# Reordering the Strassen sums in a two-layer gelu kernel: a late gelu, T3 behind T4, and an earlier split of a weight piece

## The chip, the cores and the metric

The kernel runs on one core of a Trainium2 chip. The metric is device time in microseconds (us), the median of several runs; the lower the better. TensorE is called PE (PEld is its weight load), VectorE DVE, ScalarE ACT, GpSimd POOL and SyncE SP.

## The reference, cut to what matters

A causal convolution of seven taps per head runs over the sequence, and its result goes through two matrix products with a gelu between.

```python
# x: (8, 4096, 192), weight: (8 heads, 7 taps); taps softmaxed per head
out = np.einsum('hk,bskhg->bshg', w, x_unf)        # the convolution
x = out.reshape(32768, 192)
h = x @ w_in                                       # 192 -> 2048
g = h * (1.0 / (1.0 + np.exp(-1.702 * h)))         # the gelu
return (g @ w_out).astype(np.float32)              # 2048 -> 192
```

All is in float32. The weights come as 64-bit floats: the kernel takes them apart as pairs of 32-bit words and puts float32 values together ("split", "join" and "round" below).

## The kernel before

The tokens are cut into 32 large blocks ("big"), each of two steps: a first one (s even) and a second one (s odd). The first block is done in a plainer way (`first_steps`); the other 31 run in a loop of pairs of steps, and nearly all of the time is spent there. A pair has four stages: the hidden layer of the first step, that of the second, the output of the first, the output of the second. DVE computes the convolution of a later block in the spaces between: `work(t)` takes the next pieces of that from a list, as many as fit into t us by the kernel's own estimates.

Both layers are computed by schemes that trade products for sums. The hidden layer takes 21 products ("terms") where the plain way takes 24. Each goes into one of four PSUM buffers (called x, y, z and sums here), with pieces copied aside (k15 to k20, all in one SBUF tile `room`). The output layer is a Strassen scheme: seven products (A11 B11, A12 B21, S4 B22, A22 T4, S1 T1, S2 T2, S3 T3) in place of eight. A and S come from w_out. B11 to B22 are gelu outputs in the tile `g`, and T1 to T4 are differences of them, made by DVE. T1 and T2 lie in the memory of k15, k20, k19 and k18. T3 overwrites B12 and T4 overwrites B21. Each has two halves (u = 0, 1).

```python
def half(s, b, u):
    if b in (T1, T2):
        return room[:, 2 * (b - T1) + u, :].rearrange("p (f t) -> p f t", t=T)
    return g[:, s % 2, u, b, :, :]
...
def sum_g(s, u, dst, terms):                                            # L494
    vec.tensor_sub(half(s, dst, u), half(s, terms[0], u), half(s, terms[1], u))
def sum_1(s, u): sum_g(s, u, T1, (B12, B11))
def sum_2(s, u): sum_g(s, u, T2, (B22, T1))
def sum_3(s, u): sum_g(s, u, T3, (B22, B12))
def sum_4(s, u): sum_g(s, u, T4, (T2, B21))
```

The hidden layer of a step; `pe(slot, *terms)` issues the matmuls of terms (each 2 x 2 matmuls of 64 rows, seen as eight records in the profile: L472), and `gelu` is an ACT instruction (L487):

```python
def hidden(s, x, z, y, sums, work, fetch):
    second = s % 2
    ...
    if second:
        pe(z, 7, first=True)
    pe(sums, 12)
    act.copy(k15, sums)                       # L524
    pe(x, 5, 17)
    gelu(s, B11, 0, x)
    if not second:
        pe(z, 7, first=True)
    pe(sums, 0)
    act.copy(k16, sums)                       # L530
    work(3.2 if second else 1.5)
    pe(y, 6, 14, first=True)
    vec.tensor_sub(x, z, k15)                 # L533
    work(2.6)
    pe(sums, 13)
    act.copy(k19, sums)                       # L536
    pe(x, 2)
    act.copy(k18, x)                          # L538
    pe(z, 11)
    pe(sums, 20, 10)
    vec.tensor_sub(k15, y, k19)               # L541
    gelu(s, B12, 0, sums)
    pe(x, 4)
    act.copy(k20, x)                          # L544
    vec.tensor_sub(k19, z, k19)               # L545
    work(1.1)
    gelu(s, B22, 1, k19)
    gelu(s, B22, 0, k15)
    pe(y, 8)
    pe(sums, 1, 9, first=True)
    pe(y, 15)
    if second:
        sum_1(s - 1, 0)
    else:
        work(1.2)
    work(1.1)
    vec.tensor_add(k20, k20, sums)            # L557
    vec.tensor_sub(k16, y, k16)               # L558
    gelu(s, B11, 1, k20)
    pe(x, 18)
    gelu(s, B21, 1, x)
    fetch()                                   # term 16 of the next step, into z
    if not second:
        act.copy(y, z)                        # L565
    gelu(s, B21, 0, k16)
    if second:
        sum_2(s - 1, 0)
    else:
        work(1.2)
    pe(sums, 3, 19)
    work(0.7)
    vec.tensor_add(k18, k18, sums)            # L573
    gelu(s, B12, 1, k18)                      # the "last gelu"
```

The output of a step. `product2` is 64 matmuls (L582) in 16 groups of four: three column tiles of one product and, as the fourth, a third of another product. `quarters` (L598) makes the last third of A22 T4. The results are added up and turned (L618) for the store.

```python
def output(s, ra, rb, work, between=None):
    ...
    p1, p3c = product2(s, ra, 0, (A11, B11), (S4, B22, 0))
    act.copy(u1, p1)
    act.copy(chunk(p3, 0), p3c)
    sum_1(s, 1)
    sum_2(s, 1)
    sum_3(s, 0)
    sum_3(s, 1)
    work(0.7)
    p2, p3c = product2(s, rb, 0, (A12, B21), (S4, B22, 1))
    act.copy(chunk(p3, 1), p3c)               # L654
    vec.tensor_add(u2, u1, p2)                # L655
    out.turn(0, 0, u2)
    sum_4(s, 0)
    sum_4(s, 1)
    p6, p3c = product2(s, ra, 1, (S2, T2), (S4, B22, 2))
    act.copy(chunk(p3, 2), p3c)
    vec.tensor_add(u2, u1, p6)                # L661
    work(3.2)
    ...
    p5, p4c = product2(s, rb, 1, (S1, T1), (A22, T4, 0))
    q = quarters(s, rb, 0, A22, T4, 2)
    ...                                       # L667 to L672, a turn
    if s % 2:
        work(1.5)
    else:
        sum_1(s + 1, 0)
        sum_2(s + 1, 0)
    p7, p4c = product2(s, ra, 0, (S3, T3), (A22, T4, 1))
    ...                                       # L680 to L684, two turns, the store
```

At the start, the four pieces of w_in are taken apart by DVE (L273, L274, L295, L300, L304) and ACT (L284 and, by the value of LATE, three steps L289 to L291 or, with one more clamp on DVE, L276, one step L287), between the first plain products:

```python
LATE = 4                                      # pieces from here on take the clamp on DVE
...
    gelu(0, B11, 0, slots[0])
    gelu(0, B12, 0, sums)
    for m, n, slot, b in quarters[2:]:
        plain(0, 0, m, n, slot)
        gelu(0, b, 0, slot)
    cross(0, 1, C11, C21, nc.gpsimd)
    split_piece(3)
    split_rest(3)
    round_w_in(2)
    load_w_out(2)
    split_piece(4)
    split_rest(4)
    join_piece(3)
    round_w_in(3)
    load_w_out(3)
```

The whole kernel:

Of the kernel before, what the change touches and what calls it, by code (L numbers as in the profile page):

```python
# [15 lines left out]
def kernel(  # L16
# [72 lines left out]
    def load_x(big):  # L89


        p, c = divmod(big, CHUNKS)
        xin = xins[big] = xin_pool.tile([P, 2, NJ, XW], F32, name="xin")
        if c == 0:
            nc.gpsimd.memset(xin[0:R, :, 0, :], 0.0)
        for n in range(2):
            for o in range(2):
                j = 1 if c == 0 and o == 0 else 0
                t = c * TOK + o * T + (j - 1) * Q
                for v in range(2):  # L100
                    q0 = o * R + v * Q
                    nc.sync.dma_start(
                        out=xin[q0 : q0 + Q, n, j:NJ, :],
                        in_=x_v[n, p, t : t + (NJ - j) * Q, v * Q : v * Q + XW].rearrange(
                            "(j i) d -> i j d", i=Q
                        ),
                    )
# [3 lines left out]
    sums = psum.tile([P, 2, TOK], F32, name="sums")  # L111
# [3 lines left out]
    B11, B12, B21, B22, T1, T2 = range(6)  # L115
# [6 lines left out]
    k15, k20, k19, k18, k16 = (room[:, i, :].rearrange("p (h n) -> p h n", h=2) for i in range(5))  # L122
# [138 lines left out]
    def words(i):  # L261
        w = raw[i % NW].rearrange("p (n w) -> p n w", w=2)
        return (w[:, :, 0], w[:, :, 1]) + tuple(sets[SET[i]])


    LATE = 4

    def split_piece(i):

        lo, hi, m, l, e = words(i)  # L270
        ef = e.bitcast(F32)

        vec.tensor_scalar(m, hi, 0xFFFFF, 1 << 20, op0=ALU.bitwise_and, op1=ALU.bitwise_or)  # L273
        vec.tensor_scalar(e, hi, 20, 0x7FF, op0=ALU.logical_shift_right, op1=ALU.bitwise_and)  # L274
        if i >= LATE:
            vec.tensor_scalar(  # L276
                ef, e, float(LOW + 255), float(LOW), op0=ALU.min, op1=ALU.max
            )

    def split_rest(i):  # L280

        lo, hi, m, l, e = words(i)
        ef = e.bitcast(F32)
        act.activation(l.bitcast(F32), lo, AF.Copy, scale=2.0**-32)  # L284

        if i >= LATE:
            act.activation(e, ef, AF.Identity, bias=bias[:, 3:4], scale=2.0**23)  # L287
        else:
            act.activation(ef, e, AF.Relu, bias=bias[:, 0:1])  # L289
            act.activation(ef, ef, AF.Relu, bias=bias[:, 1:2], scale=-1.0)  # L290
            act.activation(e, ef, AF.Identity, bias=bias[:, 2:3], scale=-(2.0**23))  # L291
# [40 lines left out]
    def load_w_out(i):  # L332
        nc.sync.dma_start(
            out=raw[i].rearrange("p (c d) -> p c d", c=CW),
            in_=w_out_v[:, i * CW : (i + 1) * CW, :],
        )
# [149 lines left out]
    def gelu(s, b, u, src):  # L486
        act.activation(  # L487
            half(s, b, u).rearrange("p f t -> p (f t)"),
            src.rearrange("p h n -> p (h n)"),
            AF.Gelu_apprx_sigmoid,  # L490
        )

    def sum_g(s, u, dst, terms):
        vec.tensor_sub(half(s, dst, u), half(s, terms[0], u), half(s, terms[1], u))  # L494

    def sum_1(s, u):
        sum_g(s, u, T1, (B12, B11))

    def sum_2(s, u):
        sum_g(s, u, T2, (B22, T1))  # L500

    def sum_3(s, u):
        sum_g(s, u, T3, (B22, B12))
# [6 lines left out]
        for k in ks:  # L510
            product1(slot, NC * (2 * u + m) + k, 2 * k + n, s, k == first)

    def hidden(s, x, z, y, sums, work, fetch):

        second = s % 2

        def pe(slot, *ts, first=False):
            terms(s, slot, *ts, first=first)
# [9 lines that stand above are left out]
            pe(z, 7, first=True)  # L528
        pe(sums, 0)
        act.copy(k16, sums)  # L530
        work(3.2 if second else 1.5)
        pe(y, 6, 14, first=True)
        vec.tensor_sub(x, z, k15)  # L533
# [15 lines that stand above are left out]
        pe(y, 8)  # L549
        pe(sums, 1, 9, first=True)  # L550
        pe(y, 15)
        if second:
            sum_1(s - 1, 0)
        else:
            work(1.2)
        work(1.1)
        vec.tensor_add(k20, k20, sums)  # L557
        vec.tensor_sub(k16, y, k16)  # L558
        gelu(s, B11, 1, k20)
        pe(x, 18)  # L560
        gelu(s, B21, 1, x)
        fetch()
        if not second:

            act.copy(y, z)  # L565
        gelu(s, B21, 0, k16)
        if second:
            sum_2(s - 1, 0)
        else:
            work(1.2)  # L570
        pe(sums, 3, 19)
        work(0.7)
        vec.tensor_add(k18, k18, sums)  # L573
        gelu(s, B12, 1, k18)

    def product2(s, slot, bank, ab, last, first=True):

# [59 lines left out]
    def chunk(t, c):  # L637
        return t[c * Q : (c + 1) * Q, :]

    def output(s, ra, rb, work, between=None):  # L640

        out = Out(s)
        u1, u2, p3, p4 = us

        p1, p3c = product2(s, ra, 0, (A11, B11), (S4, B22, 0))
        act.copy(u1, p1)
        act.copy(chunk(p3, 0), p3c)
        sum_1(s, 1)
        sum_2(s, 1)
        sum_3(s, 0)  # L650
        sum_3(s, 1)
        work(0.7)
        p2, p3c = product2(s, rb, 0, (A12, B21), (S4, B22, 1))
        act.copy(chunk(p3, 1), p3c)  # L654
        vec.tensor_add(u2, u1, p2)  # L655
# [3 lines that stand above are left out]
        p6, p3c = product2(s, ra, 1, (S2, T2), (S4, B22, 2))  # L659
        act.copy(chunk(p3, 2), p3c)  # L660
        vec.tensor_add(u2, u1, p6)  # L661
        work(3.2)
        if between:
            between()
        p5, p4c = product2(s, rb, 1, (S1, T1), (A22, T4, 0))
        q = quarters(s, rb, 0, A22, T4, 2)
        act.copy(chunk(p4, 0), p4c)  # L667
        vec.tensor_add(u1, u2, p5)
        act.copy(chunk(p4, 2), q[2])
        vec.tensor_add(p3, u1, p3)  # L670
        for l in (0, 1, 3):
            vec.tensor_add(chunk(p4, 2), chunk(p4, 2), q[l])  # L672
        out.turn(0, 1, p3)
# [6 lines that stand above are left out]
        act.copy(chunk(p4, 1), p4c)  # L680
        vec.tensor_add(u1, u1, p7)
        vec.tensor_add(u2, u2, p7)
        out.turn(1, 1, u1)
        vec.tensor_sub(u2, u2, p4)  # L684
        out.turn(1, 0, u2)
        out.store()
# [3 lines left out]
    def work(us):  # L690
        while todo and todo[0][1] <= us + 0.2:
            us -= todo[0][1]
            todo.pop(0)[2]()
# [28 lines left out]
    def first_steps(fetch):  # L722

        first, second = slice(0, 1), slice(1, 2)
# [49 lines left out]
        plain(0, 0, 0, 0, slots[0], (2,))  # L774
        plain(0, 0, 0, 1, sums, (2, 0), 1)
        gelu(0, B11, 0, slots[0])
        gelu(0, B12, 0, sums)
        for m, n, slot, b in quarters[2:]:
            plain(0, 0, m, n, slot)
            gelu(0, b, 0, slot)  # L780
        cross(0, 1, C11, C21, nc.gpsimd)
        split_piece(3)
        split_rest(3)
        round_w_in(2)
        load_w_out(2)
        split_piece(4)
        split_rest(4)
        join_piece(3)
        round_w_in(3)
        load_w_out(3)  # L790
        load_x(1)

        def piece_5():
# [61 lines left out]
    def fetch(s, slot):  # L855

        need(f"first {s // 2}")
        terms(s, slot, 16, first=True)
# [6 lines left out]
    x, y, z = slots[2], slots[1], slots[0]  # L865
    for big in range(1, N_BIG):
        s = 2 * big
        more = big + 1 < N_BIG
        hidden(s, x, z, y, sums, work, lambda: fetch(s + 1, z))
        give(s)  # L870
        x, z, y, sums = z, x, sums, y
        hidden(s + 1, x, z, y, sums, work, lambda: fetch(s + 2, z) if more else None)
        if more:
            act.copy(sums, z)
        output(s, y, x, work)
        if more:
            need(f"all {big + 1}")
            cross(big + 1, 1)
        if big + 2 < N_BIG:
            todo.extend(prepare(big + 2))  # L880
        output(s + 1, x, y, work)
        x, y, z = z, x, y
# [30 lines left out]
```

## Time and profile before

| | |
|---|---|
| time, median of 3 runs | 2425.85 us (2425.5 to 2426.86) |
| span in the profile | 2424.7 us |
| PE busy | 2391.2 us |
| DVE busy | 2018.8 us |
| ACT busy | 1052.7 us |
| granted PE clock, mean | 0.999 |

How to read it: an engine's row gives its busy time, its share of the span and its number of instructions. A row of waits says which engine and line waited for which other, then the total, the number of times and the longest, in us. A row of a time line gives start, duration, engine, line, operation, and output <- inputs; a bracket at its end holds the idle time before it and what ended it. A row of the chain of waits gives start, duration, and what was running. Matmuls are pipelined, and their ends are modelled. L-numbers are lines of the kernel, as marked in the code above; in the changed kernel they shift by a line or two.

### The profile page before, as it was taken

How to read it: one execution, taken by the hardware profiler on the slowest of the kernel's cores; microseconds unless marked ns; L12 is line 12 of the kernel's file. 1: busy time of each engine (PE TensorE's matmuls, PEld its weight loads, DVE VectorE, ACT ScalarE, POOL GpSimd, SP SyncE). 2: the span in 40 equal slices, each digit the busy share in tenths (PEclk: the TensorE clock that was granted, in tenths of full speed). 3: DMA queues.
4: the chain of work that ended last, by engine and by line, in shares of the span. 5: the costliest groups of instructions: out<-in, count | busy, mean ns of one | idle time of the engine just before them, and what ended most of it. 6: DMA issues, size and time to landing. Idle time of an engine off the chain costs nothing.

```text
span 2424.7 us, 71778 instructions
## 1 busy us (share of the span) xinstructions
PE 2391.2 (99%) x32602; PEld 1755.3 (72%) x32602; DVE 2018.8 (83%) x2853; ACT 1052.7 (43%) x1369; POOL 9.1 (0%) x30
## 2 busy tenths in 40 slices
PE   9999999999999999999999999999999999999998
PEld 8667776677776777766777667777677776677765
DVE  7888888888888889888888888888888988888866
ACT  6235443344433455333544334443345533354433
POOL 1000000000000000000000000000000000000000
PEclk9999999999999999999999999999999999999999
DMA  7421332212323123322133231232312323213210
GB/s 163 84 52 35 64 67 56 62 35 51 67 56 65 37 47 67 62 58 50 36 64 67 56 62 32 54 67 54 65 37 46 67 60 61 52 34 65 43 29 15
DMA packets 195824, 135.90 MB, mean 56 GB/s; under 512 B 110752, under 2 KB 186016, under 8 KB 193536
## 3 DMA queue, kind: packets, MB, share of 16 engines
q1 hardware_dynamic: 194912, 131.06, 26.6%
q8 instruction: 255, 4.18, 0.8%
q14 instruction: 49, 0.40, 0.1%
q10 hardware_dynamic: 560, 0.13, 0.0%
q0 software_dynamic: 48, 0.13, 0.0%
HBM read 53.15 MB, written 25.17 MB: 32 GB/s over the span
## 4 chain that ended last, share of the span: by engine, by line
PE 73%; DVE 15%; ACT 6%; issue 3%; DMA 2%; SPq 1%; POOL 0%; DVEq 0%; POOLq 0%; ACTq 0%
PE slot L472 30%; PE slot L582 20%; PE sums L472 11%; PE sums L582 9%; DVE room L494 4%; ACT g L487 4%; DVE g L494 3%; DMA out_dram<-osbs 2%; DVE osbs L618 2%; PE slot L598 2%; DVE room L557 1%; ACT room L544 1%; DVE room L672 1%; DVE xt L396 1%; SPq L633 1%
## 5 line engine op out<-in xcount | busy, mean ns | idle before, releaser
L472 PE MATMUL slot<-crossed,w_in_s 64*128 64x256 f32 x3940 | 904.9, 378 | 7.3 <-DVE room L557 7.3
L472 PE MATMUL slot<-f,w_in_s 64*128 64x256 f32 x3940 | 905.1, 378 | 1.6 <-DVE w_in_s L304 1.6
L582 PE MATMUL slot<-g,w_out_s 128*32 128x256 f32 x9792 | 781.5, 379 | 9.0 <-DVE g L494 9.0
L472 PEld LDWEIGHTS slot<-crossed,w_in_s 64*128 64x128 f32 x3940 | 731.4, 187 | 60.0 <-DVE room L557 15.7
L472 PEld LDWEIGHTS slot<-f,w_in_s 64*128 64x128 f32 x3940 | 731.5, 187 | 54.7 <-issue 9.0
L582 PEld LDWEIGHTS slot<-g,w_out_s 128*32 128x32 f32 x9792 | 422.8, 110 | 227.6 <-DVE g L494 18.5
L413 DVE SCALAR_TENSOR_TENSOR f<-xt,cw,f 128x512 f32<-128x512 f32 (+1 forms) x570 | 421.9, 740 | 15.6
L582 PE MATMUL sums<-g,w_out_s 128*32 128x256 f32 x4704 | 385.6, 379 | 5.1 <-DVE g L494 5.1
L487 ACT ACTIVATE g<-room 128x1024 f32<-128x1024 f32 x310 | 321.3, 1059 | 132.6 <-DVE room L557 105.2
L472 PE MATMUL sums<-crossed,w_in_s 64*128 64x256 f32 x1460 | 360.6, 378 | 2.7 <-DVE room L557 2.7
L472 PE MATMUL sums<-f,w_in_s 64*128 64x256 f32 x1460 | 360.6, 378 | 0.0
L582 PE MATMUL slot<-room,w_out_s 128*32 128x256 f32 x4032 | 305.2, 379 | 0.0
L472 PEld LDWEIGHTS sums<-crossed,w_in_s 64*128 64x128 f32 x1460 | 270.5, 187 | 25.7 <-DVE room L557 6.7
L582 PEld LDWEIGHTS sums<-g,w_out_s 128*32 128x32 f32 x4704 | 205.0, 110 | 111.9 <-DVE g L494 10.2
L472 PEld LDWEIGHTS sums<-f,w_in_s 64*128 64x128 f32 x1460 | 270.6, 187 | 18.7 <-issue 4.5
L494 DVE TENSOR_TENSOR room<-g 128x1024 f32<-128x1024 f32 x126 | 151.2, 1200 | 106.1 <-ACT g L487 106.1
L582 PEld LDWEIGHTS slot<-room,w_out_s 128*32 128x32 f32 x4032 | 163.7, 110 | 91.6 <-issue 0.3
L487 ACT ACTIVATE g<-slot 128x1024 f32<-128x1024 f32 x157 | 159.8, 1018 | 97.9 <-PE slot L472 97.6
L494 DVE TENSOR_TENSOR room<-g,room 128x1024 f32<-128x1024 f32 x126 | 154.1, 1223 | 5.5
L582 PE MATMUL sums<-room,w_out_s 128*32 128x256 f32 x2016 | 154.5, 379 | 0.0
L494 DVE TENSOR_TENSOR g<-g 128x1024 f32<-128x1024 f32 x126 | 148.3, 1218 | 0.0
L494 DVE TENSOR_TENSOR g<-room,g 128x1024 f32<-128x1024 f32 x126 | 145.8, 1195 | 0.0
(170 smaller groups left out, 1943.7 us busy)
## 6 DMA issues: line engine op xcount, KB each, us to landing
xin<-in_x_dram SPq DMA_DIRECT2D x240, 180.0 KB, 5.0
crossed<-f SPq DMA_DIRECT2D x31, 832.0 KB, 5.9
out_dram<-osbs SPq DMA_DIRECT2D x382, 64.0 KB, 1.8
crossed<-f SPq DMA_DIRECT2D x31, 448.0 KB, 3.8
crossed<-f SPq DMA_DIRECT2D x31, 256.0 KB, 2.9
crossed<-f SPq DMA_DIRECT2D x31, 128.0 KB, 2.2
xin<-in_x_dram SPq DMA_DIRECT2D x16, 160.0 KB, 4.3
g<-in_moe_w_in_dram SPq DMA_DIRECT2D x4, 384.0 KB, 13.1
```

What stands on the lines that cost most here:

```text
L396: vec.transpose(xts[big][:, c, ns, :].rearrange("p n (j t) -> p (n j) t", t=Q), xins[big][:, ns, :, :].rearrange("p n j d -> p (n j) d")[: ...
L413: vec.scalar_tensor_tensor(out=dst, in0=src, scalar=tap, in1=dst, op0=ALU.mult, op1=ALU.add)
L472: nc.tensor.matmul(slot[:, h, j * T : (j + 1) * T], w_in_s[halves[h], a, j * P : (j + 1) * P], (f if h == o else crossed)[halves[h], b, :] ...
L487: act.activation(half(s, b, u).rearrange("p f t -> p (f t)"), src.rearrange("p h n -> p (h n)"), AF.Gelu_apprx_sigmoid,)
L494: vec.tensor_sub(half(s, dst, u), half(s, terms[0], u), half(s, terms[1], u))
L544: act.copy(k20, x)
L557: vec.tensor_add(k20, k20, sums)
L582: nc.tensor.matmul(dst[l * Q : (l + 1) * Q, :], w_out_s[:, a, j, c * Q : (c + 1) * Q], half(s, b, j // (NK // NU))[:, j % (NK // NU), :], ...
L598: nc.tensor.matmul(dst[l], w_out_s[:, a, j, c * Q : (c + 1) * Q], half(s, b, j // (NK // NU))[:, j % (NK // NU), :], start=(i == 0), stop= ...
L618: vec.transpose(self.osb[:, n, :, m * Q : (m + 1) * Q], src.rearrange("p (j t) -> p j t", t=Q),)
L633: (act if c % 2 and self.s == N_ST - 1 else nc.sync).dma_start(out=rows[c], in_=self.osb[c * Q : (c + 1) * Q, n, :, :])
L672: vec.tensor_add(chunk(p4, 2), chunk(p4, 2), q[l])
```

## The change

The sums T1 to T4 and the last gelu of a step change places in the instruction streams; their number stays. In a pair, `hidden` of the first step returns its last gelu instead of issuing it, and the second step issues it after its second copy, where ACT has time. The first half of T1 of the first step moves behind the additions to k20 and k16 in the second step, the first half of T2 into the first step's output. In each output, T3 moves behind T4. The `work` amounts are moved with them. At the start, the fourth piece of w_in (number 3) is split with the clamp on DVE, ahead of three gelus instead of behind them. The purpose is to have each producer ready before PE asks for it.

```diff
-    LATE = 4
+    LATE = 3
...
-    def hidden(s, x, z, y, sums, work, fetch):
+    def hidden(s, x, z, y, sums, work, fetch, last=lambda: None):
...
         act.copy(k16, sums)
+        last()
         work(3.2 if second else 1.5)
...
         pe(y, 15)
-        if second:
-            sum_1(s - 1, 0)
-        else:
-            work(1.2)
-        work(1.1)
+        work(2.3)
         vec.tensor_add(k20, k20, sums)
         vec.tensor_sub(k16, y, k16)
...
         if second:
-            sum_2(s - 1, 0)
+            sum_1(s - 1, 0)
         else:
             work(1.2)
         pe(sums, 3, 19)
         work(0.7)
         vec.tensor_add(k18, k18, sums)
-        gelu(s, B12, 1, k18)
+        return lambda: gelu(s, B12, 1, k18)
...
         act.copy(chunk(p3, 0), p3c)
+        if s % 2 == 0:
+            sum_2(s, 0)
         sum_1(s, 1)
         sum_2(s, 1)
-        sum_3(s, 0)
-        sum_3(s, 1)
-        work(0.7)
+        work(0.7 if s % 2 else 1.5)
...
         vec.tensor_add(u2, u1, p6)
-        work(3.2)
+        sum_3(s, 0)
+        sum_3(s, 1)
+        work(0.7)
...
         gelu(0, B11, 0, slots[0])
+        split_piece(3)
+        split_rest(3)
         gelu(0, B12, 0, sums)
         for m, n, slot, b in quarters[2:]:
             plain(0, 0, m, n, slot)
             gelu(0, b, 0, slot)
         cross(0, 1, C11, C21, nc.gpsimd)
-        split_piece(3)
-        split_rest(3)
         round_w_in(2)
         load_w_out(2)
-        split_piece(4)
-        split_rest(4)
         join_piece(3)
         round_w_in(3)
         load_w_out(3)
+        split_piece(4)
+        split_rest(4)
...
-        hidden(s, x, z, y, sums, work, lambda: fetch(s + 1, z))
+        last = hidden(s, x, z, y, sums, work, lambda: fetch(s + 1, z))
         give(s)
         x, z, y, sums = z, x, sums, y
-        hidden(s + 1, x, z, y, sums, work, lambda: fetch(s + 2, z) if more else None)
+        hidden(s + 1, x, z, y, sums, work, lambda: fetch(s + 2, z) if more else None, last)()
```

## The prediction

> **What bounds the kernel now.** I read the page first, for the balance of the engines.
>
> ```profile
> PE 2391.2 (99%) x32602; PEld 1755.3 (72%) x32602; DVE 2018.8 (83%) x2853; ACT 1052.7 (43%) x1369; POOL 9.1 (0%) x30
> ```
>
> TensorE (PE) is the bound, VectorE (DVE) is next, and 33 us of the 2424.7 us span seem to be all that PE idles. Then the list of waits, for PE alone: what holds it?
>
> ```profile
> PE slot L582 <- DVE g L494: 9.0, 19, 0.5
> PE slot L472 <- DVE room L557: 7.3, 21, 1.1
> PE sums L582 <- DVE g L494: 5.1, 10, 0.8
> PE sums L472 <- DVE room L557: 2.7, 10, 0.3
> PE slot L472 <- DVE w_in_s L304: 1.6, 1, 1.6
> ```
>
> Two waits come once per pair (19 + 10 and 21 + 10 times), one once at the start. They add up to only 25.7 us, but a matmul is shown 0.38 us long where the next group starts 0.216 us after it, so the list understates a gap. I therefore measure from start to start in the time line. The pair of steps that starts at 1002.23 is followed by the next at 1076.84: 74.61 us. Its own work, from pieces of the chain of waits that run without a gap: 42 terms at 0.864 (two take 1.73), ten products at 3.45 and two sets of quarters at 0.86, 72.5 us. So 2.1 us of each pair are lost, and 31 pairs make 65 us. Where? First loss, in the second step's hidden part (chain of waits):
>
> ```profile
> 1031.16 1.02 ACT g L487
> 1032.19 0.90 ACT room L544
> 1033.09 1.91 ACT g L487 x2
> 1035.02 1.23 DVE room L494
> 1036.25 1.14 DVE room L557
> 1037.43 2.00 PE slot L472 x16
> ```
>
> The L494 at 1035.02 is sum_1(s-1, 0). It writes T1 into the memory of k15, so it waits for the gelu that reads k15 (until 1035.0). DVE has idled 3.44 us, but L557, which frees `sums` for terms 3 and 19 and needs only the k20 copy (done at 1033.09), stands behind it. PE's last matmul before was at 1036.78; unhindered the next would start at 1037.00, not 1037.43: 0.43 us, and 0.10 more for the restart, whose second gap is 0.31 instead of 0.21.
>
> Second loss, in the output of the second step (time line of DVE, then of PE):
>
> ```profile
> 1061.62 1.18 DVE L494 TENSOR_TENSOR room<-g 128x1024 f32<-128x1024 f32 x1
> 1062.83 1.23 DVE L494 TENSOR_TENSOR room<-g,room 128x1024 f32<-128x1024 f32 x1
> 1063.97 2.36 DVE L494 TENSOR_TENSOR g<-g 128x1024 f32<-128x1024 f32 x2
> 1066.25 0.77 DVE L396 STREAM_TRANSPOSE xt<-xin 128x576 f32<-128x576 f32 x1
> 1066.94 0.38 DVE L655 TENSOR_TENSOR room<-room,sums 96x256 f32<-96x256 f32 x1
> 1067.35 0.44 DVE L618 STREAM_TRANSPOSE osbs<-room 96x256 f32<-96x256 f32 x1
> 1067.72 2.31 DVE L494 TENSOR_TENSOR g<-room,g 128x1024 f32<-128x1024 f32 x2
> ```
>
> ```profile
> 1067.88 0.61 PE L582 MATMUL sums<-room,w_out_s 128*32 128x256 f32 x6
> 1068.95 0.40 PE L582 MATMUL sums<-g,w_out_s 128*32 128x256 f32 x1 [0.47 <-DVE g L494]
> ```
>
> DVE makes T1, T2, then T3 (g<-g), and only then T4 (g<-room,g), whose first half is ready at 1068.9. But p5 starts at 1067.88 and mixes T4 into every fourth matmul: PE gets six done, then stands until 1068.95. This also leaves a trace at the end of p7: the groups of four column tiles are shifted, and two matmuls remain that run one by one.
>
> ```profile
> 1001.70 0.59 PE L582 MATMUL slot<-g,w_out_s 128*32 128x256 f32 x2
> 1002.23 0.48 PE L472 MATMUL sums<-f,w_in_s 64*128 64x256 f32 x1
> ```
>
> From p5's start at 1067.88 to the next pair at 1076.84 are 8.96 us. The work is 16 + 4 + 16 groups at 0.2157 us, 7.77, and 0.10 for the change of tile shape; 1.09 us are lost. (The first step's p5, whose T4 was ready 1 us early at 1048.9, shows no such shift.)
>
> Third and small: at 1023.95 PE loses 0.10 at term 0 of the second step, because the copy to k15 (ACT, 1022.89 to 1023.88) queued behind the first step's last gelu, which waits for DVE.
>
> **The Trainium skill.** "Perfetto Trace Analysis", Identifying the Most-Contended Engine, calls matmul occupancy a poor measure because pipelined instructions overlap; the trace agrees (0.38 shown, 0.216 apart), and I use it. "TensorEngine Tiling (Array Packing)", Key Properties, says that tiles load and multiply independently and that a change of mode drains the array. The trace agrees: four 128x32 matmuls start per 0.216 us, one left alone takes as long, and each change between the two layers costs about 0.1 us, which the new kernel keeps. "TensorE: Matmul & The Clock Gate", Architectural detail, calls ACT and DVE strict FIFOs; the 3.44 us idle ahead of sum_1 with runnable work behind it fits.
>
> **The change, part by part.** No instruction of weight is added; the matmuls are the same, so PE's own 72.5 us per pair stay. What counts is whether each producer is now early enough.
>
> (a) *sum_1(s-1, 0) behind L557.* L557 can run when DVE is free and k20 is copied. The new order puts more of the convolution before it: after L545 (odd step, ends at 1031.5) come one tap (0.77) and seven sums (2.7 us, as at 1026.3 to 1029.0), so L557 runs from about 1035.0 to 1036.2. Term 3 is due at about 1036.9. Early by 0.7. The 0.54 us go.
>
> (b) *The late gelu.* In the second step ACT now has: copy y (until 1020.6), gelu B21, then the k15 copy as soon as term 12 is done (about 1022.4 to 1023.4), ahead of 1023.85. Then gelu B11, k16 copy, and the late gelu at about 1026.0 to 1027.0, in a gap that ACT had (1.52 us idle before 1027.71). Its reader, sum_1(s, 1), is far off. The 0.10 us go.
>
> (c) *T3 behind T4.* In the second step's output DVE now does T1 and T2 of the second half (2.4 us), one transpose (0.7), then waits for p2, adds u2 and turns (0.8), then T4. From p2's end to the first half of T4 I take the first step's figures: p2 ends at 1046.47, T4's half at 1048.9, 2.46 us, against 3.45 us for p6. So 1.0 us early, if DVE is free by p2's end + 0.4: it gets there about 0.4 us before that. In the first step there is one T sum more ahead of T4 (sum_2), against two taken away. T3 follows p6: its halves are ready 2.0 and 3.2 us after p6's end, and p7 starts 4.3 us after it. The 1.09 us go.
>
> (d) *The fourth piece of w_in.* Its two ACT steps (0.91 + 0.92) go ahead of three gelus. Now its words are ready at 38.38 and L304 ends at 39.37, and PE stands from 37.54 to 39.51: 1.97, of which 0.21 is normal. With the new order: gelu to 31.0, ACT steps to about 32.8, join beside them, L300 and L304 to 34.9. PE needs it at 37.7. The other gelus come 0.8 us later, the tightest being that on `sums` at 33.7, needed at about 35.1. With its restart, 1.84 us go.
>
> The sum: 0.54 + 1.09 + 0.10 = 1.73 us per pair, a period of 72.9 us. 29 pairs make 50. The first pair, 75.6 long, gives about 2.1: there the order leaves five sums of w_in (2 us) behind the output, so the first L533 comes about 0.6 us late for term 2. The last gives 1.9 (its L557 wait is 1.3 long). With 1.8 at the start: 56 us. 2425.85 - 56 = 2370.
>
> **The rivals.** *The list of waits is right and the rest is not recovered:* 25.7 us, 2400. For it speaks that the profiler says so; against it the start-to-start gaps, above all the shifted tail, which the output with no T4 wait (the last before the pairs, ending at 105.5) doesn't show. *DVE becomes the bound:* the reduced filling in the outputs (0.7 + 3.2 + 0.7 + 3.2 + 1.5 before, 0.7 + 1.5 + 0.7 + 0.7 + 1.5 after) moves up to 3 us of convolution into the hidden parts. DVE idles 3.44 us there, and its load of 83% of 74.6 is 62 us against a period of 72.9. Were it late, L557 would cost half a microsecond per pair again: 2386. *A tight handover gets a hiccup:* the copy to k15 ends some 0.4 us ahead of its use; the k16 copy is as close today (1026.2 against 1026.6) and costs nothing. If it does: 0.1 per pair, 2373. *A new wait outweighs the gain* (the T sums late for p7 or for WAR on k16, k18, k19): I found margins of 0.6 us and more, all else behind by at least one product; 2430 or more would need 1.9 us per pair.
>
> **Range and chances.** The work left per pair is fixed and the repeats lie within 1.4 us, so downwards there is little: 2366. Upwards a residue of 0.35 us per pair gives 2381. The 2% mark is 2377.3, 7 us over the centre, or 0.24 us per pair. Faster by over 2%: 0.80; within 2%: 0.18; slower: 0.02.
>
> **What would show it.** The period from pair to pair 72.9 us; no PE wait for g from the T4 sum nor for room from the add to k20, nor the wait on w_in at 37.5; groups of four to the end of p7. A period near 73.4 means that the tail shift stays; near 74, that T4 is late still. A new line in PE's waits, above all one on ACT, would make me wrong; so would a first pair much over 74 us.

## The result, and the profile after

The changed kernel takes 2369.84 us, median of 6 runs (2369.46 to 2369.95), where the kernel before takes 2425.68 (6 runs beside them): a ratio of 0.9769 (95% interval 0.9756 to 0.9781), 55.8 us less. The prediction said 2370. The granted PE clock is 0.999 to 1.0 in every run of both kernels, so it has no part in this.

The page of the changed kernel, the balance of the engines and the shares of the chain of waits:

```profile
PE 2359.7 (100%) x32602; PEld 1754.3 (74%) x32602; DVE 2027.2 (86%) x2854; ACT 1048.0 (44%) x1367; POOL 9.1 (0%) x30
...
PE 99%; DVE 0%; POOL 0%; DMA 0%; issue 0%; SPq 0%; ACT 0%; POOLq 0%; DVEq 0%; ACTq 0%
```

The number of matmuls is the same, and PE's busy time fell by 31.5 us: part of what looked busy before was standing. The chain that ended last is now nearly all PE. PE's waits on other engines, in full:

```profile
PE sums L375 <- POOL osbs masks.py:199: 1.4, 1, 1.4
PE slot L472 <- DVE slot L535: 0.5, 1, 0.5
PE slot L386 <- POOL bias L259: 0.5, 1, 0.5
```

Of the five waits shown of before none is left; L535 (L533 before) is a new one, once, in the first pair. The pair from 978.63 to 1051.49 lasts 72.86 us, against 74.61. The DVE rows that answer to those of before, in the second step's output (the T sums are L494 in both kernels; `room` output is T1 or T2, g<-room,g is T4, g<-g is T3):

```profile
1037.35 1.18 DVE L494 TENSOR_TENSOR room<-g 128x1024 f32<-128x1024 f32 x1
1038.57 1.23 DVE L494 TENSOR_TENSOR room<-g,room 128x1024 f32<-128x1024 f32 x1
1039.71 0.77 DVE L396 STREAM_TRANSPOSE xt<-xin 128x576 f32<-128x576 f32 x1
1040.86 0.42 DVE L654 TENSOR_TENSOR room<-room,sums 96x256 f32<-96x256 f32 x1 [0.38 <-ACT room L653]
1041.31 0.44 DVE L616 STREAM_TRANSPOSE osbs<-room 96x256 f32<-96x256 f32 x1
1041.68 2.31 DVE L494 TENSOR_TENSOR g<-room,g 128x1024 f32<-128x1024 f32 x2
1044.31 0.42 DVE L660 TENSOR_TENSOR room<-room,slot 96x256 f32<-96x256 f32 x1 [0.32 <-ACT room L659]
1044.65 2.35 DVE L494 TENSOR_TENSOR g<-g 128x1024 f32<-128x1024 f32 x2
```

The addition of p2 (L654) came 2.5 us after the next product's start before the change (1066.94, where p6 starts at 1064.42), and now 0.71 us after it. DVE is free at 1040.48 and stands for 0.38 us; by the bracket it waits for ACT's copy (L653) of the third of S4 B22 that was made beside p2. T4's first half is there at about 1042.9, and T3 follows in the shadow of p5. PE at the start of p5 (time line):

```profile
1043.61 0.39 PE L580 MATMUL sums<-room,w_out_s 128*32 128x256 f32 x3
1043.63 0.38 PE L580 MATMUL sums<-g,w_out_s 128*32 128x256 f32 x1
1043.82 0.39 PE L580 MATMUL sums<-room,w_out_s 128*32 128x256 f32 x3
```

Three of (S1, T1) and one of T4 in each group from the first group on: no six in a row, no wait.

### The profile page after: what moved, and what is told of

Read it like the earlier page. It is cut to its first block, busy times and chain, and to the rows that moved or that the text cites. A ratio compares the mean times of both kernels' runs of the same rounds, so it can differ in the third digit from the quotient of the medians.

```text
span 2368.1 us, 71902 instructions
## 1 busy us (share of the span) xinstructions
PE 2359.7 (100%) x32602; PEld 1754.3 (74%) x32602; DVE 2027.2 (86%) x2854; ACT 1048.0 (44%) x1367; POOL 9.1 (0%) x30
## 4 chain that ended last, share of the span: by engine, by line
PE 99%; DVE 0%; POOL 0%; DMA 0%; issue 0%; SPq 0%; ACT 0%; POOLq 0%; DVEq 0%; ACTq 0%
PE slot L472 36%; PE slot L580 31%; PE sums L580 15%; PE sums L472 13%; PE slot L596 2%; PE sums L596 1%; PE slot L710 1%; DMA out_dram<-osbs 0%; POOL osbs L246 0%; DVE osbs L616 0%; PE sums L375 0%; PE slot L386 0%; DVE room L673 0%; DVE slot L535 0%; DVE w_in_s L319 0%
## 5 line engine op out<-in xcount | busy, mean ns | idle before, releaser
L580 PE MATMUL slot<-g,w_out_s 128*32 128x256 f32 x9792 | 770.9, 379 | 0.0
L494 DVE TENSOR_TENSOR room<-g,room 128x1024 f32<-128x1024 f32 x126 | 154.1, 1223 | 5.5
L494 DVE TENSOR_TENSOR room<-g 128x1024 f32<-128x1024 f32 x126 | 150.9, 1197 | 0.0
L494 DVE TENSOR_TENSOR g<-g 128x1024 f32<-128x1024 f32 x126 | 148.0, 1214 | 0.0
L494 DVE TENSOR_TENSOR g<-room,g 128x1024 f32<-128x1024 f32 x126 | 145.7, 1194 | 0.0
```

The source lines that it names most:

```text
L580: nc.tensor.matmul(dst[l * Q : (l + 1) * Q, :], w_out_s[:, a, j, c * Q : (c + 1) * Q], half(s, b, j // (NK // NU))[:, j % (NK // NU), :], ...
```

## The experiments

**Undo one part at a time.** The base is the changed kernel, 2369.84 us. Each run is compared with it as the difference of medians; both were measured beside the kernel before.

*T3 ahead of T4 again.*

```diff
         sum_2(s, 1)
+        sum_3(s, 0)
+        sum_3(s, 1)
         work(0.7 if s % 2 else 1.5)
...
         vec.tensor_add(u2, u1, p6)
-        sum_3(s, 0)
-        sum_3(s, 1)
         work(0.7)
```

> The changed kernel with T3 put back ahead of T4 in both outputs (the rest of the change stays). Theory of the prediction: in the second step's output the first half of T4 comes again 1.07 us after PE could use it, and the whole lateness is lost, because the column tile of T4 ends that much later: 1.09 us per pair, 30 pairs and 0.4 for the last, 33 us in all: 2403, period 73.95. Rival, only what the list of waits names (14 us) is lost: 2384, period 73.3. Rival, the gain came from elsewhere: 2370.

Measured: 2402.68 (ratio to the kernel before 0.9903, 0.9890 to 0.9917), 32.8 us more, period 73.94. PE's waits in that run:

```profile
PE slot L580 <- DVE g L494: 9.0, 19, 0.5
PE sums L580 <- DVE g L494: 5.0, 10, 0.7
```

The list names 14.0 us (14.1 before the change), and 32.8 were lost. The rival that trusts the list falls.

*sum_1 ahead of the addition to k20 again.*

```diff
         work(2.3)
+        if second:
+            sum_1(s - 1, 0)
         vec.tensor_add(k20, k20, sums)
...
-        if second:
-            sum_1(s - 1, 0)
-        else:
+        if not second:
             work(1.2)
```

> The changed kernel with the first half of the first step's T1 back ahead of the addition to k20 in the second step. Theory: DVE waits for the gelu on k15 again, terms 3 and 19 come 0.44 late and 0.10 goes to the restart, 0.54 per pair, some more in the first and last pair: 17 to 18 us, 2387, period 73.4. Rival, only the 10 us that the list of waits names: 2380. Rival, the sum itself costs nothing there: 2370.

Measured: 2387.40 (0.9841, 0.9828 to 0.9855), 17.6 us more, period 73.40, with the same two gaps of before in a pair (0.44 ahead of term 3 and 0.10 after it); the last pair loses 1.40. The waits listed are 6.6 and 2.8, again about half of the loss. One row of DVE and one of PE from the pair that starts at 985.67:

```profile
1018.33 1.22 DVE L494 TENSOR_TENSOR room<-g 128x1024 f32<-128x1024 f32 x1 [0.34 <-ACT g L487]
1020.75 0.48 PE L472 MATMUL slot<-crossed,w_in_s 64*128 64x256 f32 x1 [0.27 <-DVE room L557]
```

The 2.3 us of filling now stand ahead of the sum and shrink DVE's idle time from 3.44 to 0.34 us. The sum still starts with the gelu, 32.7 us after the pair's start (32.8 before the change), and PE is as late as before: it is the sum's place that costs, not DVE's load.

*The last gelu in its own place.*

```diff
-        return lambda: gelu(s, B12, 1, k18)
+        gelu(s, B12, 1, k18)
+        return lambda: None
```

> The changed kernel with the first step's last gelu issued in its own place again. Theory: the copy to k15 ends at the moment at which PE wants term 0, 0.10 us per pair: 3 us, 2373, period 72.96. Rival, with the other parts changed ACT has room enough and nothing is lost: 2370. Rival, the gelu holds up more than term 0 (copy to k16, term 13): 0.3 us per pair and more, 2379.

Measured: 2374.46 (0.9788, 0.9774 to 0.9801), 4.6 us more, against 3 expected. The period is 72.99, so 0.13 per pair: 0.10 at term 0 and 0.02 just ahead of it. The first pair takes 74.41 instead of 73.71, where DVE is behind, so that the gelu's data are late and the copy to k15 behind it holds PE for 0.6 us more. The ACT rows of a later pair of that run show the queue: the gelu (1000.47) waits for DVE, the copy L525 stands behind it. In the changed kernel PE's data release that copy 20.23 us after the pair's start; here it starts at 20.67.

```profile
1000.47 1.06 ACT L487 ACTIVATE g<-room 128x1024 f32<-128x1024 f32 x1 [0.38 <-DVE room L571]
1001.44 0.99 ACT L525 COPY room<-slot 128x1024 f32<-128x1024 f32 x1
```

*The fourth piece of w_in behind the gelus.* This restores LATE = 4 and the old order of the start.

```diff
-    LATE = 3
+    LATE = 4
...
-        split_piece(3)
-        split_rest(3)
         gelu(0, B12, 0, sums)
...
+        split_piece(3)
+        split_rest(3)
         round_w_in(2)
         load_w_out(2)
+        split_piece(4)
+        split_rest(4)
         join_piece(3)
         round_w_in(3)
         load_w_out(3)
-        split_piece(4)
-        split_rest(4)
```

> The changed kernel with the fourth piece of w_in split behind the three gelus again, without the clamp on DVE. Theory: PE stands 1.8 us more at 37 us, 2371.7; nothing else moves. Rival, later slack takes it up: 2369.9. Rival, it delays the pieces of w_out too: 2373 or more.

Measured: 2371.96 (0.9776, 0.9763 to 0.9790), 2.1 us more. PE's wait on `w_in_s` is back (1.6 in the list), and every pair lasts as long as in the changed kernel: no slack later on takes anything up. From the first product with w_in to the first pair of the loop it takes 83.67 us here and 81.83 in the changed kernel, 1.84 more. The other 0.3 lies ahead of that product, which starts anywhere from 21.1 to 22.5 us in the eleven traces.

*One part alone.* The three other parts undone together, T3 behind T4 kept.

```diff
+            sum_1(s - 1, 0)            # ahead of the addition to k20, as above
...
+        gelu(s, B12, 1, k18)           # in its own place, as above
...
+    LATE = 4                           # and the old order of the start
```

> The kernel with T3 behind T4 (and sum_2 in the first step's output) as the only part of the change; the gelu, sum_1 and the w_in piece stand as before. Theory, the parts are independent: 2369.8 + 17.5 + 3.1 + 1.8 = 2392, period 73.5. Rival, they overlap (the gelu and sum_1 delay the same engine): 2385 or, if each makes the other's wait longer, 2400.

Measured: 2394.42 (0.9870, 0.9856 to 0.9885), 24.6 us over the changed kernel. The three undone singly cost 17.6 + 4.6 + 2.1 = 24.3. So the parts add up: each took a gap of its own away. With T3's 32.8 the four make 57.1, and the whole change saved 55.8. The rest of the change (the first half of T2 in the first step's output, and the new `work` amounts) was not undone by itself; the sum leaves nothing for it.

**How late may T4 be?** The prediction saw PE stand in p5 and two matmuls left over at the end of p7, and took these for losses that could part (a period near 73.4 for the shift alone, near 74 for a late T4). Are they two effects, or one lateness seen twice? DVE got small extra work ahead of T4 in the second step's output: additions and transposes done again with the same result.

```diff
         vec.tensor_add(u2, u1, p2)
         out.turn(0, 0, u2)
+        if s % 2:
+            vec.tensor_add(u2, u1, p2)     # delay_0
+            out.turn(0, 0, u2)             # delay_1: these two
+            vec.tensor_add(u2, u1, p2)     # delay_2: all three
```

> The changed kernel with one addition done twice on DVE ahead of T4 in the second step's output (0.42 us more work with the same result). T4's first half then comes 0.3 us before PE can use it, by the time line. All theories: nothing lost, 2369.8, unless a handover needs more than 0.3 us: then 0.1 to 0.2 per pair, 2373 to 2376.

> As before, with the addition and the transpose done twice (0.82 us): T4's first half comes about 0.1 us after PE could use it. Theory A, what is lost is T4's lateness, to the next group of matmuls (0.216): 0.1 to 0.2 per pair, 3 to 7 us, 2373 to 2377. Theory B, a late T4 always costs the two matmuls that are left over at the end of p7 (0.43): 13 us, 2383. Theory C, only a wait that the list shows counts: 2370.

> As before, with the addition done three times and the transpose twice (1.25 us): T4's first half comes about 0.5 us late. Theory A: 0.5 to 0.65 per pair, 16 to 20 us, 2386 to 2390, most of it with no wait in the list. Theory B: 0.43 and a gap of up to 0.1: 2383 to 2386. Theory C: under 3 us, 2370 to 2373.

Measured, with the end of T4's first half and the start of the first T4 matmul, both counted from the start of p5 (medians over the pairs of each trace):

| kernel | T4 half ready | first T4 matmul | period | over the shortest | time |
|---|---|---|---|---|---|
| changed | -0.75 | 0.02 | 72.86 | | 2369.84 |
| delay_0 | -0.27 | 0.02 | 72.86 | 0 | 2369.99 |
| delay_1 | 0.17 | 0.23 | 73.09 | 0.23 | 2377.47 |
| delay_2 | 0.66 | 0.71 | 73.58 | 0.72 | 2391.87 |
| T3 ahead | 1.03 | 1.08 | 73.94 | 1.08 | 2402.68 |

In all three rows with a loss it exceeds the delay of that first matmul (0.21, 0.69, 1.06) by no more than 0.03 us. Single pairs that deviate follow the same line: one of delay_1 whose first T4 matmul starts at 0.31 lasts 73.17, one of T3 ahead with 0.42 lasts 73.28, two of delay_2 with 0.79 last 73.65. A fixed cost of the leftover (theory B, 0.43) falls with delay_1. Only a listed wait counting (theory C) falls too: in delay_1 the list of PE's waits has no such entry at all, and 7.6 us are lost; in delay_2 it has this one line for a loss of 22.0 us:

```profile
PE slot L580 <- DVE g L494: 0.4, 2, 0.2
```

Both entries belong to the two pairs with 0.79. The six records of (S1, T1) fill the first 0.61 us of p5 on PE, so a T4 matmul at 0.71 shows as a gap of only 0.10, and the list does not have those; at 1.08 it shows as 0.47. The list for the weight loads (PEld) comes nearer, but is no measure either: it names 28.8 us for L494 with T3 ahead (32.8 lost), 18.3 in delay_2 (22.0 lost) and 0.2 in delay_1 (7.6 lost), and for L557 with sum_1 ahead 21.8, more than the 17.6 lost.

Theory A stands in its slope, though not in its rounding to whole groups of 0.216. Both results lie above its ranges, delay_1 by 0.5 us and delay_2 by 2, because the lateness was more than I had counted (0.69 and not 0.5 in delay_2). The time line of PE in delay_1 shows how a wait hides. First the start of p5:

```profile
1047.29 0.61 PE L580 MATMUL sums<-room,w_out_s 128*32 128x256 f32 x6
1047.52 0.40 PE L580 MATMUL sums<-g,w_out_s 128*32 128x256 f32 x1
1047.72 0.39 PE L580 MATMUL sums<-room,w_out_s 128*32 128x256 f32 x3
```

A float32 matmul of the program is two records on PE (the code has 32 in a product, the profile 64). So the three column tiles of (S1, T1) have two passes each to do, six records, while the fourth waits for T4. From there on that tile runs one group behind the others. PE never stands, but at the end of p7 one matmul is left over. The last row of p7 in delay_1, and in the changed kernel:

```profile
1055.10 0.38 PE L580 MATMUL slot<-g,w_out_s 128*32 128x256 f32 x1
```

```profile
1051.16 0.40 PE L580 MATMUL slot<-g,w_out_s 128*32 128x256 f32 x4
```

So the next pair starts 0.23 us later.

**The wait of the first pair.** The first pair of the changed kernel lasts 73.71 us: the sums of w_in that the shorter `work` left over hold DVE, and PE waits 0.69 us (start to start) at term 2, with 0.10 for the restart.

```diff
         sum_3(s, 0)
         sum_3(s, 1)
-        work(0.7)
+        work(1.5 if between else 0.7)      # between: only the output before the first pair
```

> The changed kernel with 1.5 instead of 0.7 us of work behind T3 in the output that comes before the first pair, so that fewer sums of w_in are left over behind it. Theory: the first L535 comes 0.8 us earlier, and the PE wait of the first pair (0.69 and 0.10) goes: 0.8 us, 2369.0. Rival: the sums delay the additions behind p5 there instead, and nothing is gained: 2369.8 or more.

Measured: 2368.89 (2368.72 to 2369.92; 0.9767, 0.9753 to 0.9780). The wait on L535 is gone from the list, and the first pair takes 72.93. By the trace 0.78 us are won; the medians differ by 0.95, and the intervals overlap by far, so the times alone would not settle it.

## Why the prediction was right, point by point

- *What bounds.* PE, with 2.1 us lost per pair by start-to-start counting. Right: 1.76 of them could be had (74.62 to 72.86). What is left is 72.5 us of work, which no part touched, and 0.34 us at the two changes between the layers (by the time line 0.12 at the one and 0.22 at the other, where the prediction spoke of about 0.1 each).
- *(a) sum_1 behind L557.* 0.54 per pair predicted; undoing it cost 0.54 in the period (73.40 less 72.86) and 17.6 us. The addition to k20 ended at 1012.2, and term 3 was due at 1013.3: early by 1.1, where I had counted 0.7.
- *(b) The late gelu.* 0.10 per pair predicted; undoing it cost 0.13, and 0.7 in the first pair. The mechanism was right, the term a little small.
- *(c) T3 behind T4.* 1.09 predicted, 1.08 measured. The margin was 0.75 us instead of 1.0: I had counted p2's end from the chain (1046.47), where by the time line the next product starts at 1046.29. The working saw a gap and a leftover and took them for separable; the delays show that both are one thing, T4's lateness. The number was right because it had been counted from p5's start to the next pair, over both.
- *(d) The piece of w_in.* 1.84 predicted. The loop of pairs starts 2.31 earlier (105.80 to 103.49), but 0.44 of that lies ahead of the first product with w_in, where the change does nothing yet. From that product to the first pair it is 83.70 before and 81.83 after: 1.87.
- *First and last pair.* 2.1 and 1.9 predicted. The first became 1.90 shorter (75.61 to 73.71), with the wait for term 2 that was foreseen at 0.6 (it is 0.69 and 0.10). From the start of the last pair to the last matmul it is 71.69 against 73.64: 1.95.
- *The sum.* The 29 pairs between first and last give 50.4 (28 at 1.76 and one, whose T4 had been only 0.42 late, at 1.10); with 1.90, 1.95 and 1.87 that is 56.2, against 56 predicted and 55.8 measured. The terms were right, but that the total came so close is luck: the start alone moves by 1.4 us from trace to trace.
- *The rivals.* The list of waits as the measure of the loss fell in four runs (T3 ahead, sum_1 ahead, delay_1 and delay_2). DVE did not become the bound: its share rose from 83% to 86% of a shorter span, and it still stands at many places (93.9 us in all ahead of L654). By the amounts that the prediction lists, the outputs gave up 4.2 us of filling (9.3 to 5.1) and not 3; there was room for that too. The close handover of k15 got no hiccup (the copy L525 leaves no gap at term 0). No new wait came except that of the first pair.

## What to carry to other kernels

Count what an engine loses from start to start against its clean pieces; a list of waits counts only the time in which it stands altogether, and here it named 25.7 us of 56. When one operand of interleaved matmuls is made by another engine, look at the end of that stretch too: a leftover of single matmuls says that one column tile ran behind, though nothing ever waited visibly. On an in-order queue an instruction that will wait belongs behind all that could run now and that somebody needs sooner.

## What I had not expected of the hardware

With four column tiles in use, an operand that is 0.2 us late for one of them costs 0.23 us per pair and leaves no wait and no gap where it arrives. At the three delays measured, 0.21, 0.69 and 1.06 us, the loss is equal to the delay within 0.03 us, although PE's listed wait reads nothing at 0.21 and about 0.5 at 1.06 (14.0 us in 29 entries). And a T4 that was ready 0.27 us ahead of p5's start cost nothing at all: the handover from DVE to PE was not dearer than that.
